# A delta-rule kernel's triangular inverse: from 128x128 products to 64x64 tiles on the array's diagonal

## The chip, the core and the metric

The kernel runs on one core of a Trainium2 chip. The core has a matrix engine (TensorE, PE in the profile, with its weight loads listed apart as PEld), three engines for elementwise work (VectorE or DVE, ScalarE or ACT, GpSimd or POOL) and queues that issue DMAs (here all on SyncE, SP). Each engine works through its own instructions in order, and semaphores tie the engines together. The metric is the device time of one execution in microseconds (us).

## The reference

Four batch elements, eight heads, 768 tokens, 48 values a head. First a delta rule runs along the tokens of each head, with a state S of 48x48 that starts at zero:

```
k_n = k / (norm(k) + 1e-6)
for t in tokens:
    y[t]  = q[t] @ S
    S     = S + beta[t] * outer(k_n[t], v[t] - k_n[t] @ S)
```

The heads' outputs, put side by side, form x of 768x384 for each batch element. Two mixers follow: h = relu(x^T @ w_tok1) @ w_tok2 along the tokens (256 hidden), u = x + h^T, and out = u + relu(u @ w_ch1) @ w_ch2 along the channels (1536 hidden). The mixers' weights come as doubles; everything is computed in float32.

## The kernel before

**The delta rule in chunks.** The 768 tokens of a batch element are cut into six chunks of 128, 24 chunks in all. In a chunk with start state S0, with kb = beta k and L the strictly lower triangle of kb k^T (128x128 for each head), the kernel solves (I + L) u = beta v - kb S0, and then y = q S0 + tril(q k^T, -1) u and S1 = S0 + k^T u.

**The inverse.** T = (I + L)^-1 is built by doubling. With T right for diagonal blocks of s, blocks of 2s follow from T <- T - T L_off T, where L_off holds the blocks below the diagonal that join two blocks of s. The matrix engine takes its left operand (the stationary one, loaded as weights) transposed, so both T (tile t_t) and its transpose W (tile w_t) are kept, 128 partitions by 8 heads by 128 columns. The grams lie in gm, where gm[:, h, 0] is L transposed.

**prep(t)**, lines 237 to 351, does what needs no state. It scales the keys (lines 244 to 268), transposes keys, queries and scaled keys on the matrix engine (p_t, line 276), forms the grams (p_g, line 288, two row tiles of 64 partitions, one for even and one for odd heads) and masks them on DVE into gm (line 292). For blocks of 2, POOL fills w_t with the identity (line 303), masks the gram into off (line 307) and subtracts (line 311); eight transposes (p_w, line 318) and two ACT copies (line 319) make t_t from w_t. Then comes a loop over s = 2, 4, 8, 16, 32, 64. Each step multiplies L by the first-half columns of T (p_l, line 330, eight heads, 128x128 weights against 64 columns), masks the product on DVE into lt (line 331), multiplies lt by the second-half columns of W (p_wu, line 339), and w_t by lt (p_x, line 343, not in the last step), and subtracts the products on DVE from t_t (line 344) and w_t (line 347). A step's p_l waits for the update of t_t of the step before, and p_wu for lt.

**recur(t)**, lines 353 to 407, walks the chunk through the state: p_b, p_u (which reads w_t), p_s, the state's update, p_y. **mixer(b)**, lines 409 to 471, does both mixers of a batch element once its six chunks are done: p (line 416), p_h (428), transposes p_ut (439), p_c (450) with a relu on ACT (455), p_o (462), and the result's addition and DMA (469, 470). **load_weights** rounds the doubles to float32 in 34 pieces, with five or six DVE operations and one POOL addition (line 190) a piece.

**The order.** Each of these functions is a generator that yields between pieces. A heap (lines 480 to 507) takes the pieces by due time: a chunk's preparation takes the unit of time before its recurrence, and a batch element's mixers are spread over the six units after its last chunk. So the first six chunks have no mixer beside them, the other 18 have, and the last batch element's mixer stands alone at the end. The framework's scheduler takes that order as a priority and may move an instruction ahead of one whose inputs it does not expect in time; each engine's order is then fixed in the program. PSUM tiles come from three rings: att (three slots: p_t, p_g, p_w, p_l, p_wu, p_x), seq (two) and mlp (three).

Of the kernel before, what the change touches and what calls it, by code (L numbers as in the profile page):

```python
# [9 lines left out]
FP32 = mybir.dt.float32  # L10
# [4 lines left out]
C = 128   # tokens in a chunk  # L15
DP = 64   # partitions a head takes in the transposed keys and queries
WP = 384  # weights of a partition that are rounded at a time
# [3 lines left out]
def kernel(  # L21
# [24 lines left out]
    on the chip to the nearest float32, the widest type its engines multiply.  # L46
    """
    nc = tc.nc
# [11 lines left out]
    GT = 256            # tokens in a group of the channel mixer  # L60
# [13 lines left out]
    def ps_att(shape, name):  # L74
        return psum.tile(shape, FP32, name=name, tag="att", bufs=3)
# [22 lines left out]
    mask_1 = const.tile([128, 64], FP32, name="mask_1")  # L98
    nc.gpsimd.memset(mask_1, 1.0)
    for sign in (1, -1):  # L100
        nc.gpsimd.affine_select(
            out=mask_1, in_=mask_1, pattern=[[-2 * sign, 64]], base=0,
            channel_multiplier=sign, compare_op=ALU.is_ge, fill=0.0,
        )
    # the other steps, on L T: rows in the second half of their own block of 2s
    SIZES = [2, 4, 8, 16, 32, 64]
    masks = {}
    for s in SIZES:
        m = const.tile([128, 64 // s, s], FP32, name=f"mask_{s}")
# [9 lines left out]
        masks[s] = m  # L119

    # masked L T of a step; the first-half columns are written, the rest stay 0
    lt_buf = {}
    for s in SIZES[:-1]:
        lt_buf[s] = const.tile([128, H, 128], FP32, name=f"lt_{s}")
# [12 lines left out]
    # state, two heads to a block-diagonal block  # L137
# [99 lines left out]
    def prep(t):  # L237
        """What needs no state: scaled keys, masked grams and the inverse."""
# [64 lines left out]
        nc.gpsimd.tensor_copy(  # L303
            out=w_t, in_=ident[:, None, :].to_broadcast([128, H, 128])
        )
        off = work.tile([128, H, 64], FP32, name="off", bufs=1)
        nc.gpsimd.tensor_tensor(  # L307
            out=off, in0=gm[:, :, 0, 1::2],
            in1=mask_1[:, None, :].to_broadcast([128, H, 64]), op=ALU.mult,
        )  # L310
        nc.gpsimd.tensor_tensor(  # L311
            out=w_t[:, :, 1::2], in0=w_t[:, :, 1::2], in1=off, op=ALU.subtract
        )
        yield
        for g in range(H // 4):
            p_t = ps_att([128, 4, 128], "p_w")
            for i in range(4):
                nc.tensor.transpose(p_t[:, i], w_t[:, 4 * g + i], ident)  # L318
            nc.scalar.copy(t_t[:, 4 * g : 4 * g + 4], p_t)
        yield  # L320

        for s in SIZES:
            last = s == SIZES[-1]
            lt = lt_buf[s]
            lt_e = lt[:, :, None, :] if last else pairs(lt, s)[:, :, :, 0]
            t_e = pairs(t_t, s)[:, :, :, 0]
            w_o = pairs(w_t, s)[:, :, :, 1]
            p_l = ps_att([128, H, 64], "p_l")
            for h in range(H):
                nc.tensor.matmul(p_l[:, h], gm[:, h, 0], t_e[:, h])  # L330
            nc.vector.tensor_tensor(  # L331
                out=lt_e, in0=halves(p_l, s),
                in1=masks[s][:, None].to_broadcast([128, H, 64 // s, s]), op=ALU.mult,
            )
            yield
            rows = 64 if last else 128
            p_w = ps_att([rows, H, 64], "p_wu")
            for h in range(H):
                nc.tensor.matmul(p_w[:, h], lt[:, h], w_o[:, h])  # L339
            if not last:  # L340
                p_x = ps_att([128, H, 64], "p_x")
                for h in range(H):
                    nc.tensor.matmul(p_x[:, h], w_t[:, h], lt_e[:, h])  # L343
                nc.vector.tensor_tensor(  # L344
                    out=t_e, in0=t_e, in1=halves(p_x, s), op=ALU.subtract
                )
            nc.vector.tensor_tensor(  # L347
                out=w_o[:rows], in0=w_o[:rows], in1=halves(p_w, s), op=ALU.subtract
            )
            yield  # L350
        ready[t] = (kp, kbq_t, gm, w_t, bv)

    def recur(t):
        """The chunk's walk through the state."""
# [54 lines left out]
    def mixer(b):  # L409
        """Both mixers on a batch element; xb is x, then u = x + h."""  # L410
# [62 lines left out]
    # ---- order of issue: a chunk's recurrence beside the next chunk's  # L473
    # preparation and the mixers of the batch element before ----
# [20 lines left out]
    n_prep = 1 + 3 + H // 4 + 2 + 2 * len(SIZES)  # L495
# [42 lines left out]
```

## Time and profile before

| what | value |
|---|---|
| median of 3 runs | 1697.59 us (1691.23 to 1698.04) |
| the profiled execution, first to last instruction | 1689.6 us |
| PE busy, with 10350 matmuls | 1588.7 us |
| PEld busy, with 10350 weight loads | 1395.2 us |
| DVE busy | 513.9 us |
| ACT busy | 176.7 us |
| POOL busy | 173.8 us |
| mean granted clock of PE | 0.917 |

The profiled execution is known by its span alone; what lies around the span is in the runs' times. A row of a group reads: line of the kernel, engine, operation, output tile <- input tiles, shape, count, then busy time in us and mean ns of one, then the idle time of the engine just before and what ended most of it. For a matmul 128*64 128x64 means 128 weight rows by 64 weight columns, and 64 moving columns on 128 partitions. A row of the order in time reads: start in us, length in us from the first start to the last end, engine, line, operation, tiles, shape, count. The length of one matmul in the trace includes its way through the array, so it is longer than the distance between two starts. The granted clock is 1.00 at full speed.

### The profile page before, as it was taken

How to read it: one execution, taken by the hardware profiler on the slowest of the kernel's cores; microseconds unless marked ns; L12 is line 12 of the kernel's file. 1: busy time of each engine (PE TensorE's matmuls, PEld its weight loads, DVE VectorE, ACT ScalarE, POOL GpSimd, SP SyncE). 2: the span in 40 equal slices, each digit the busy share in tenths (PEclk: the TensorE clock that was granted, in tenths of full speed). 3: DMA queues.
4: the chain of work that ended last, by engine and by line, in shares of the span. 5: the costliest groups of instructions: out<-in, count | busy, mean ns of one | idle time of the engine just before them, and what ended most of it. 6: DMA issues, size and time to landing. Idle time of an engine off the chain costs nothing.

```text
span 1689.6 us, 22914 instructions
## 1 busy us (share of the span) xinstructions
PE 1588.7 (94%) x10350; PEld 1395.2 (83%) x10350; DVE 513.9 (30%) x920; ACT 176.7 (10%) x407; POOL 173.8 (10%) x188
## 2 busy tenths in 40 slices
PE   5888989889899999999999999999999999999999
PEld 4888888888888988888888889879878879888776
DVE  6464643212123232223223222222233232222100
ACT  1000101001011101101100101110110101010111
POOL 5031211001011011101100100110110110000000
PEclk9995757567589999999999999999999999999999
DMA  4131210000000000001000000010000000000000
GB/s 115 38 77 45 71 47 15 5 10 19 0 6 20 5 15 15 10 11 24 11 15 10 15 15 10 15 24 6 15 20 5 10 10 1 6 5 1 10 10 19
DMA packets 83377, 33.02 MB, mean 20 GB/s; under 512 B 75824, under 2 KB 78896, under 8 KB 83280
## 3 DMA queue, kind: packets, MB, share of 16 engines
q1 hardware_dynamic: 83280, 31.56, 7.6%
q8 instruction: 81, 1.33, 0.3%
q14 instruction: 16, 0.13, 0.0%
HBM read 26.84 MB, written 4.72 MB: 19 GB/s over the span
## 4 chain that ended last, share of the span: by engine, by line
PE 90%; DVE 5%; POOL 3%; issue 1%; ACT 0%; POOLq 0%; DVEq 0%
PE p_l L330 18%; PE p_wu L339 17%; PE p_x L343 15%; PE p_o L462 11%; PE p_c L450 10%; PE p_g L288 3%; PE p_u L372 3%; PE p_y L402 2%; PE p_t L276 2%; PE p_h L428 2%; DVE gm L292 2%; PE p L416 1%; PE p_w L318 1%; DVE lt L331 1%; DVE t_t L344 1%; POOL off L307 1%
## 5 line engine op out<-in xcount | busy, mean ns | idle before, releaser
L330 PEld LDWEIGHTS p_l<-t_t,gm 128*128 128x128 f32 x2304 | 316.9, 218 | 54.0 <-DVE t_t L344 37.4
L330 PE MATMUL p_l<-t_t,gm 128*128 128x64 f32 x2304 | 326.4, 302 | 23.5 <-DVE t_t L344 23.1
L339 PEld LDWEIGHTS p_wu<-w_t,lt 128*128 128x128 f32 (+1 forms) x2304 | 297.4, 210 | 57.2 <-DVE lt L331 42.8
L339 PE MATMUL p_wu<-w_t,lt 128*128 128x64 f32 (+1 forms) x2304 | 306.6, 295 | 25.7 <-DVE lt L331 25.7
L343 PE MATMUL p_x<-lt,w_t 128*128 128x64 f32 x1920 | 277.4, 306 | 0.0
L343 PEld LDWEIGHTS p_x<-lt,w_t 128*128 128x128 f32 x1920 | 267.4, 223 | 0.0
L344 DVE TENSOR_TENSOR t_t<-t_t,p_x 128x512 f32<-128x512 f32 x120 | 82.5, 687 | 505.9 <-PE p_x L343 505.9
L450 PE MATMUL p_c<-u_t,wc 128*128 128x256 f32 x864 | 217.1, 388 | 0.1
L462 PE MATMUL p_o<-wc,r 128*128 128x384 f32 x576 | 208.1, 494 | 0.0
L331 DVE TENSOR_TENSOR lt<-p_l,mask 128x512 f32<-128x512 f32 x144 | 99.5, 691 | 325.6 <-PE p_l L330 325.6
L450 PEld LDWEIGHTS p_c<-u_t,wc 128*128 128x128 f32 x864 | 153.1, 190 | 20.2 <-issue 2.6
L462 PEld LDWEIGHTS p_o<-wc,r 128*128 128x128 f32 x576 | 101.5, 191 | 49.7 <-issue 1.3
L347 DVE TENSOR_TENSOR w_t<-w_t,p_wu 128x512 f32<-128x512 f32 x144 | 97.9, 680 | 33.0 <-PE p_wu L339 33.0
L292 DVE TENSOR_TENSOR gm<-p_g,mask_u 128x512 f32<-128x512 f32 x96 | 61.9, 685 | 112.3 <-PE p_g L288 111.9
L455 ACT ACTIVATE r<-p_c 128x256 f32<-128x256 f32 x144 | 55.3, 384 | 385.8 <-PE p_c L450 385.8
L265 POOL TENSOR_TENSOR bv<-v_raw,beta_t 128x384 f32<-128x384 f32 x24 | 20.2, 843 | 654.7 <-DVE rhs L367 497.6
L288 PE MATMUL p_g<-kbq_t,k_t 64*128 64x256 f32 x384 | 61.9, 412 | 9.8 <-DVE gm L292 6.7
L277 ACT COPY k_t<-p_t 128x512 f32<-128x512 f32 x24 | 14.0, 585 | 490.4 <-PE p_t L276 489.9
L288 PEld LDWEIGHTS p_g<-kbq_t,k_t 64*128 64x128 f32 x384 | 38.9, 191 | 26.1 <-DVE gm L292 10.5
L318 PE MATMUL p_w<-ident,w_t 128*128 128x128 f32 x192 | 26.9, 285 | 28.5 <-POOL w_t L311 28.5
L190 POOL TENSOR_TENSOR w_f<-w_f,w_r 128x384 uint32<-128x384 uint32 (+1 forms) x34 | 35.7, 1050 | 171.4 <-DVE w_f L182 166.7
L318 PEld LDWEIGHTS p_w<-ident,w_t 128*128 128x128 f32 x192 | 21.5, 144 | 38.1 <-POOL w_t L311 36.8
(75 smaller groups left out, 967.2 us busy)
## 6 DMA issues: line engine op xcount, KB each, us to landing
d<-in_moe_w_ch_dram SPq DMA_DIRECT2D x24, 384.0 KB, 3.1
k_raw<-in_k_dram SPq DMA_DIRECT2D x24, 192.0 KB, 2.5
qpad<-in_q_dram SPq DMA_DIRECT2D x24, 192.0 KB, 2.8
v_raw<-in_v_dram SPq DMA_DIRECT2D x24, 192.0 KB, 2.6
out_dram<-o_sb SPq DMA_DIRECT2D x24, 192.0 KB, 1.9
d<-in_moe_w_tok_dram SPq DMA_DIRECT2D x6, 256.0 KB, 3.3
d<-in_moe_w_tok_dram SPq DMA_DIRECT2D x4, 384.0 KB, 3.1
beta_sb<-in_beta_dram SPq DMA_DIRECT2D x1, 96.0 KB, 2.2
```

Source lines behind the costliest of these rows:

```text
L288: nc.tensor.matmul(p_g[par][:, jj], k_t[lo : lo + DP, j], kbq_t[lo : lo + DP, j])
L292: nc.vector.tensor_tensor(out=gm[:, 4 * g + par : 4 * g + 4 : 2], in0=p_g[par], in1=mask_u[:, None, None, :].to_broadcast([128, 2, 2, 128] ...
L318: nc.tensor.transpose(p_t[:, i], w_t[:, 4 * g + i], ident)
L330: nc.tensor.matmul(p_l[:, h], gm[:, h, 0], t_e[:, h])
L331: nc.vector.tensor_tensor(out=lt_e, in0=halves(p_l, s), in1=masks[s][:, None].to_broadcast([128, H, 64 // s, s]), op=ALU.mult,)
L339: nc.tensor.matmul(p_w[:, h], lt[:, h], w_o[:, h])
L343: nc.tensor.matmul(p_x[:, h], w_t[:, h], lt_e[:, h])
L344: nc.vector.tensor_tensor(out=t_e, in0=t_e, in1=halves(p_x, s), op=ALU.subtract)
L347: nc.vector.tensor_tensor(out=w_o[:rows], in0=w_o[:rows], in1=halves(p_w, s), op=ALU.subtract)
L450: nc.tensor.matmul(p_c, wc1[:, cb, f * 128 : (f + 1) * 128], u_t[:, cb], start=(cb == 0), stop=(cb == NCB - 1),)
L455: nc.scalar.activation(r, p_c, ACTF.Relu)
L462: nc.tensor.matmul(p_o, r2[f][:, i * C : (i + 1) * C], wc2[:, f], start=(f == 0), stop=(f == NHT - 1),)
```

## The change

The tile size R = 64 is introduced. Up to s = 16, and in the step at s = 32, every product is taken as two 64x64 products, one on partitions 0 to 63 and one on 64 to 127, which write the same partitions of the output. The operands are kept compact: w_r and t_r hold, for each partition, only the 64 columns of its own diagonal block (8 heads by 64), and the masks, the identity and the lt buffers are folded to that width at the start by POOL. T is no longer updated by a product of its own: before each step t_r is made from w_r by a DVE transpose in blocks of 32x32 (flip). The first transposes on the matrix engine and their ACT copies go. The step at 64 is written out: one more product (p_x) and a subtraction make the first block's T complete, then p_l is evacuated by ACT into lt_buf[64] and p_w by ACT, times -1, into the upper right block of w_t. The other blocks of w_t are a POOL memset of zero and two POOL copies of w_6, which is w_r. Comments are dropped, and the count of pieces in the plan follows the new pieces (20, as before).

```diff
+    def folded(name, full, width):
+        t = const.tile([128, width], FP32, name=name)
+        nc.gpsimd.tensor_copy(out=t, in_=full[:, 0:width])
+        for lo in range(width, full.shape[-1], width):
+            nc.gpsimd.tensor_tensor(
+                out=t, in0=t, in1=full[:, lo : lo + width], op=ALU.add
+            )
+        return t
...
-        w_t = work.tile([128, H, 128], FP32, name="w_t")
-        t_t = work.tile([128, H, 128], FP32, name="t_t", bufs=1)
+        w_r = work.tile([128, H, R], FP32, name="w_r", bufs=1)
+        t_r = work.tile([128, H, R], FP32, name="t_r", bufs=1)
         nc.gpsimd.tensor_copy(
...
+        for lo in range(0, 128, R):
+            nc.gpsimd.tensor_tensor(
+                out=off[lo : lo + R], in0=gm[lo : lo + R, :, 0, lo + 1 : lo + R : 2],
+                in1=mask_1[lo : lo + R, None, :].to_broadcast([R, H, R // 2]),
+                op=ALU.mult,
+            )
...
-        for g in range(H // 4):
-            p_t = ps_att([128, 4, 128], "p_w")
-            for i in range(4):
-                nc.tensor.transpose(p_t[:, i], w_t[:, 4 * g + i], ident)
-            nc.scalar.copy(t_t[:, 4 * g : 4 * g + 4], p_t)
-        yield
...
+        def flip(dst, src):
+            nc.vector.transpose(
+                dst.rearrange("p h n -> p (h n)"), src.rearrange("p h n -> p (h n)")
+            )
+
+        def step(s, size, w, t):
+            lt, half = lt_buf[s], size // 2
+            lt_e = pairs(lt, s)[:, :, :, 0]
+            t_e = pairs(t, s)[:, :, :, 0]
+            w_o = pairs(w, s)[:, :, :, 1]
+            p_l = ps_att([128, H, half], "p_l")
             for h in range(H):
-                nc.tensor.matmul(p_l[:, h], gm[:, h, 0], t_e[:, h])
+                for lo in range(0, 128, size):
+                    r = slice(lo, lo + size)
+                    nc.tensor.matmul(p_l[r, h], gm[r, h, 0, r], t_e[r, h])
             nc.vector.tensor_tensor(
                 out=lt_e, in0=halves(p_l, s),
...
+            p_w = ps_att([128, H, half], "p_wu")
             for h in range(H):
-                nc.tensor.matmul(p_w[:, h], lt[:, h], w_o[:, h])
-            if not last:
-                p_x = ps_att([128, H, 64], "p_x")
-                for h in range(H):
-                    nc.tensor.matmul(p_x[:, h], w_t[:, h], lt_e[:, h])
-                nc.vector.tensor_tensor(
-                    out=t_e, in0=t_e, in1=halves(p_x, s), op=ALU.subtract
-                )
+                for lo in range(0, 128, size):
+                    r = slice(lo, lo + size)
+                    nc.tensor.matmul(p_w[r, h], lt[r, h], w_o[r, h])
...
+        for s in SMALL:
+            if s == 32:
+                break
+            flip(t_r, w_r)
+            yield from step(s, R, w_r, t_r)
+        flip(t_r, w_r)
+        if R == 64:
+            w_6, t_6 = w_r, t_r
...
+        yield from step(32, 64, w_6, t_6)
+        lo_r, hi_r = slice(0, 64), slice(64, 128)
+        p_x = ps_att([64, H, 32], "p_x")
+        for h in range(H):
+            nc.tensor.matmul(p_x[:, h], w_6[lo_r, h], lt_buf[32][lo_r, h, 0:32])
+        nc.vector.tensor_tensor(
+            out=t_6[lo_r, :, 0:32], in0=t_6[lo_r, :, 0:32], in1=p_x, op=ALU.subtract
+        )
+        w_t = work.tile([128, H, 128], FP32, name="w_t")
+        nc.gpsimd.memset(w_t[hi_r, :, 0:64], 0.0)
+        nc.gpsimd.tensor_copy(out=w_t[lo_r, :, 0:64], in_=w_6[lo_r])
+        nc.gpsimd.tensor_copy(out=w_t[hi_r, :, 64:128], in_=w_6[hi_r])
+        yield
+        p_l = ps_att([128, H, 64], "p_l")
+        for h in range(H):
+            nc.tensor.matmul(p_l[hi_r, h], gm[lo_r, h, 0, hi_r], t_6[lo_r, h])
+        nc.scalar.copy(lt_buf[64][hi_r], p_l[hi_r])
+        yield
+        p_w = ps_att([64, H, 64], "p_wu")
+        for h in range(H):
+            nc.tensor.matmul(p_w[:, h], lt_buf[64][hi_r, h], w_6[hi_r, h])
+        nc.scalar.mul(w_t[lo_r, :, 64:128], p_w, -1.0)
+        yield
         ready[t] = (kp, kbq_t, gm, w_t, bv)
```

More of the change, by code (lines that the diff above doesn't have):

```diff
@@ L16 @@
 DP = 64
+R = 64
 WP = 384
@@ L118 @@
         )
-        masks[s] = m
+        width = (R if s < R else 64) // 2
+        masks[s] = folded(f"mask_{s}", m.rearrange("p n s -> p (n s)"), width)
+    half_of = const.tile([128, 2], FP32, name="half_of")
+    for i in range(2):
+        nc.vector.tensor_reduce(
+            out=half_of[:, i : i + 1],
+            in_=ident.rearrange("p (n two s) -> p n two s", two=2, s=32)[:, :, i],
+            axis=mybir.AxisListType.XY, op=ALU.add,
+        )
     lt_buf = {}
-    for s in SIZES[:-1]:
-        lt_buf[s] = const.tile([128, H, 128], FP32, name=f"lt_{s}")
+    for s in (2, 4, 8, 16, 32):
+        width = R if s < R else 64
+        lt_buf[s] = const.tile([128, H, width], FP32, name=f"lt_{s}")
         nc.gpsimd.memset(lt_buf[s], 0.0)
@@ L298, in prep @@
             yield
-        w_t = work.tile([128, H, 128], FP32, name="w_t")
-        t_t = work.tile([128, H, 128], FP32, name="t_t", bufs=1)
+        w_r = work.tile([128, H, R], FP32, name="w_r", bufs=1)
+        t_r = work.tile([128, H, R], FP32, name="t_r", bufs=1)
         nc.gpsimd.tensor_copy(
-            out=w_t, in_=ident[:, None, :].to_broadcast([128, H, 128])
+            out=w_r, in_=ident_r[:, None, :].to_broadcast([128, H, R])
         )
-        off = work.tile([128, H, 64], FP32, name="off", bufs=1)
@@ L313, in prep @@
+        nc.gpsimd.tensor_tensor(
+            out=w_r[:, :, 1::2], in0=w_r[:, :, 1::2], in1=off, op=ALU.subtract
         )
         yield
-        for g in range(H // 4):
-            p_t = ps_att([128, 4, 128], "p_w")
-            for i in range(4):
-                nc.tensor.transpose(p_t[:, i], w_t[:, 4 * g + i], ident)
-            nc.scalar.copy(t_t[:, 4 * g : 4 * g + 4], p_t)
-        yield
[L322 to L328, printed above, removed]
+        def flip(dst, src):
+            nc.vector.transpose(
+                dst.rearrange("p h n -> p (h n)"), src.rearrange("p h n -> p (h n)")
+            )
@@ L331, in prep @@
             nc.vector.tensor_tensor(
                 out=lt_e, in0=halves(p_l, s),
-                in1=masks[s][:, None].to_broadcast([128, H, 64 // s, s]), op=ALU.mult,
+                in1=halves(masks[s][:, None, :], s).to_broadcast(
+                    [128, H, half // s, s]
+                ),
+                op=ALU.mult,
             )
             yield
-            rows = 64 if last else 128
-            p_w = ps_att([rows, H, 64], "p_wu")
+            p_w = ps_att([128, H, half], "p_wu")
@@ L347, in prep @@
             nc.vector.tensor_tensor(
-                out=w_o[:rows], in0=w_o[:rows], in1=halves(p_w, s), op=ALU.subtract
+                out=w_o, in0=w_o, in1=halves(p_w, s), op=ALU.subtract
             )
             yield
+        for s in SMALL:
[6 more added lines that the diff above has]
+            w_6, t_6 = w_r, t_r
+        else:
+            w_6 = work.tile([128, H, 64], FP32, name="w_6", bufs=1)
+            t_6 = work.tile([128, H, 64], FP32, name="t_6", bufs=1)
+            for i in range(2):
+                c_i = slice(32 * i, 32 * i + 32)
+                nc.gpsimd.tensor_scalar_mul(w_6[:, :, c_i], w_r, half_of[:, i : i + 1])
+                nc.gpsimd.tensor_scalar_mul(t_6[:, :, c_i], t_r, half_of[:, i : i + 1])
```

23 lines of the change are left out of this document (11 added, 12 removed).

## The prediction

> **What bounds the kernel now.** I read the engines' busy times first, then the span cut where the mixers begin and end, then the groups by tile shape, and last the order of time inside one chunk in each stretch.
>
> ```profile
> span 1689.6 us, 22914 instructions
> PE 1588.7 (94%) x10350; PEld 1395.2 (83%) x10350; DVE 513.9 (30%) x920; ACT 176.7 (10%) x407; POOL 173.8 (10%) x188
> ```
> ```profile
> 42.80:484.00 441.20, 391.81 (x2096) 371.02 (x2098) 172.85 (x331) 24.85 (x51) 60.65 (x56) 0.68 0.12 32
> 484.00:1558.00 1074.00, 1048.11 (x7675) 916.70 (x7673) 305.60 (x514) 124.74 (x291) 89.78 (x84) 1.00 0.05 12
> ```
> (Columns: stretch, length, busy time and count of PE, PEld, DVE, ACT, POOL, then the granted clock, DMA share, GB/s.) TensorE bounds both stretches. From the first p_l at 42.8 us to 484 us the first six chunks run with no mixer beside them at a mean clock of 0.68; until 1558 us the other 18 run beside the mixers at 1.00, with 26 us of PE idle time in all. The last mixer follows and is not touched.
>
> ```profile
> L330 PE MATMUL p_l<-t_t,gm 128*128 128x64 f32 x2304 | 326.4, 302 | 23.5 <-DVE t_t L344 23.1 <-ACT t_t L319 0.3
> L343 PE MATMUL p_x<-lt,w_t 128*128 128x64 f32 x1920 | 277.4, 306 | 0.0
> L339 PE MATMUL p_wu<-w_t,lt 128*128 128x64 f32 x1920 | 274.1, 304 | 21.0 <-DVE lt L331 21.0
> L339 PE MATMUL p_wu<-w_t,lt 128*64 128x64 f32 x384 | 32.4, 248 | 4.7 <-DVE lt L331 4.7
> L318 PE MATMUL p_w<-ident,w_t 128*128 128x128 f32 x192 | 26.9, 285 | 28.5 <-POOL w_t L311 28.5
> ```
> These five rows are the inverse: 937 of the 1589 busy us. 2304 in L330 is 24 chunks x 6 sizes x 8 heads x 2: a float32 matmul is two weight loads and two matmuls.
>
> One step of the first stretch, the change of chunk, and the same step beside the mixers:
>
> ```profile
> 160.85 3.68 PE L330 MATMUL p_l<-t_t,gm 128*128 128x64 f32 x16 [0.78 <-DVE t_t L344]
> 165.31 3.68 PE L339 MATMUL p_wu<-w_t,lt 128*128 128x64 f32 x16 [0.78 <-DVE lt L331]
> 168.78 3.62 PE L343 MATMUL p_x<-lt,w_t 128*128 128x64 f32 x16
> 173.18 3.68 PE L330 MATMUL p_l<-t_t,gm 128*128 128x64 f32 x16 [0.78 <-DVE t_t L344]
> 177.64 1.97 PE L339 MATMUL p_wu<-w_t,lt 128*64 128x64 f32 x16 [0.78 <-DVE lt L331]
> 179.54 1.12 PE L276 MATMUL p_t<-ident,kpad 128*128 128x128 f32 x4
> ...
> 191.31 1.09 PE L318 MATMUL p_w<-ident,w_t 128*128 128x128 f32 x8
> ...
> 192.69 2.00 PE L330 MATMUL p_l<-t_t,gm 128*128 128x64 f32 x16
> ```
> ```profile
> 900.03 1.90 PE L339 MATMUL p_wu<-w_t,lt 128*128 128x64 f32 x16
> 901.76 1.95 PE L343 MATMUL p_x<-lt,w_t 128*128 128x64 f32 x16
> 903.55 1.51 PE L428 MATMUL p_h<-r,w 128*128 128x384 f32 x4
> 904.89 1.89 PE L330 MATMUL p_l<-t_t,gm 128*128 128x64 f32 x16
> 906.62 1.51 PE L428 MATMUL p_h<-r,w 128*128 128x384 f32 x4
> ...
> 938.88 1.15 PE L339 MATMUL p_wu<-w_t,lt 128*64 128x64 f32 x16
> 939.96 0.70 PE L450 MATMUL p_c<-u_t,wc 128*128 128x256 f32 x2
> ```
> In the first stretch a step takes 173.18 - 160.85 = 12.3 us, with PE waiting 0.78 us for DVE twice. Beside the mixers the waits are filled. All three groups move 64 columns; the last p_wu loads 64 weight columns in place of 128 and takes 1.15 us against 1.90. So a group is paid by its weight columns.
>
> **The clock.** It falls with the inverse alone on PE:
>
> ```profile
> 180.00:190.00 10.00, 10.00 (x66) 9.08 (x65) 8.14 (x16) 2.24 (x4) 4.70 (x5) 0.83 0.36 100
> 190.00:200.00 10.00, 9.98 (x80) 9.11 (x79) 9.94 (x17) 2.18 (x5) 5.73 (x5) 1.00 0.35 84
> 200.00:210.00 10.00, 8.44 (x47) 8.30 (x48) 5.69 (x13) 0.00 (x0) 1.00 (x1) 0.69 0.23 75
> 370.00:380.00 10.00, 8.44 (x39) 8.06 (x39) 1.98 (x3) 0.00 (x0) 0.00 (x0) 0.50 0.00 0
> ```
> If the clock is either 0.5 or 1, these means put the rise at 183.4 us and the fall at 203.8 us: full clock from 4 us to 24.3 us after the chunk's first transpose at 179.54, half clock after.
>
> [...]
>
> **The change, part by part.** (1) Up to size 16 and in the step at 32, each 128x128 product becomes two 64x64 products on the array's diagonal, with 64 weight columns and 32 moving ones: 2 tiles x 8 heads x 2 = 32 matmuls a group. (2) p_x goes from every step but the one at 32, where it is 16 matmuls on 64 rows; so do the chunk's 8 transposes (L318) and their two ACT copies. (3) In their place DVE transposes 128x512 once before each of the five steps, on the chain. (4) DVE works on 128x256 instead of 128x512. (5) The step at 64 becomes two groups of 16 matmuls of 64x64, with two ACT evacuations. So 184 matmul calls a chunk for 144, each with half the weight columns.
>
> Whether the two diagonal tiles run at once decides the price. The gram p_g is the one place where two row tiles (64 rows each) follow each other:
>
> ```profile
> 944.18 0.38 PE L450 MATMUL p_c<-u_t,wc 128*128 128x256 f32 x1
> 944.49 0.49 PE L288 MATMUL p_g<-kbq_t,k_t 64*128 64x256 f32 x2
> ```
> ```profile
> 944.49 1.13 PE L288 MATMUL p_g<-kbq_t,k_t 64*128 64x256 f32 x8
> ```
> ```profile
> 1590.78 15.54 PE p_c L450 x72
> ```
> The first pair of rows is an answer cut off at 944.50 us: two p_g matmuls had already started. Eight of 256 columns take 1.13 us in all, while p_c's 256 columns on the whole array come every 15.54 / 72 = 0.216 us, 1.73 for eight. So tiles in different rows overlap here. I take a pair at one weight load of 64 columns: a group of 16 pairs costs what 16 such matmuls cost, 1.15 us at full clock and 1.97 at half. The other bound is no overlap, 32 in a row: about 1.89 and 3.68, the old group's rows.
>
> [...]
>
> DVE, ACT and POOL prices:
>
> ```profile
> L331 DVE TENSOR_TENSOR lt<-p_l,mask 128x512 f32<-128x512 f32 x144 | 99.5, 691 | 325.6 <-PE p_l L330 325.6
> L432 DVE TENSOR_TENSOR xb<-xb,p_h 128x384 f32<-128x384 f32 x24 | 13.3, 554 | 21.0 <-PE p_h L428 20.5
> L319 ACT COPY t_t<-p_w 128x512 f32<-128x512 f32 x48 | 25.9, 588 | 64.8 <-PE p_w L318 57.0 <-issue 6.9 <-ACT ksq L245 0.9
> L307 POOL TENSOR_TENSOR off<-gm,mask 128x512 f32<-128x512 f32 x24 | 31.2, 1300 | 102.7 <-DVE gm L292 102.7
> ```
> 128 columns less cost 0.137 us, so 256 take 0.42. The DVE transpose is not in the trace; I take the 128x512 row, 0.69, between half (0.35) and double (1.38). An ACT evacuation takes 0.59. POOL's off becomes two of 64x256, about 0.65 each, the same 1.3 in sum. Its three new operations at the chunk's end (a memset, two copies to w_t) release only the recurrence, which starts behind the next chunk's transposes; uncovered, three of half the POOL row's size would cost some 2 us a chunk.
>
> Gap after p_l: 0.78 - 0.69 + 0.42 = 0.51. Gap after p_w: 0.51 + 0.69 for the transpose = 1.20; nothing but the chain's next group waits for it. A step is 2 x 1.97 + 1.71 = 5.65 at half clock and 2 x 1.15 + 1.71 = 4.01 at full. The chunk's end is p_x 1.97, gap 0.51, p_l 1.97, gap 0.68 (ACT), p_w 1.97: 7.1.
>
> **First stretch.** The same place of two chunks:
>
> ```profile
> 284.97 3.69 PE p_l L330 x16
> ...
> 359.20 3.69 PE p_l L330 x16
> ```
> 74.2 us a chunk; the first chunk's inverse is 441.2 - 5 x 74.2 = 70.2. After: the first is 0.69 + 5 x 5.65 + 7.1 = 36. The others: the head, 192.69 - 179.54 = 13.15, loses the transposes and copies (192.69 - 191.31 = 1.4) and gains 0.69 for the first transpose: 12.5. Until 24.3 us the clock is full: 11.8 / 4.01 = 2.9 steps; 2.1 more at 5.65 make 11.6; the end 7.1; 43.0 together. 36 + 5 x 43 = 251 us, 190 saved. The weights' rounding keeps DVE up to 9.94 of 10 us busy (190 to 200 us) and now lies beside shorter steps: I charge 10 us, bounds 0 and 30. Stays 180.
>
> **Beside the mixers.** The shortest of one p_wu matmul is the tail that a group's length holds beyond its starts:
>
> ```profile
> L339 PE MATMUL p_wu<-w_t,lt x109: 219/275/323, 900.0 to 960.0; 128*128 128x64 f32 x93, 128*64 128x64 f32 x16
> ```
> 1074 / 18 = 59.7 a chunk. The inverse, start to start: 6 p_l x 1.73, 5 p_wu x 1.73, 5 p_x x 1.79, the last p_wu 1.08, the transposes 1.09 less the tail, 0.9: 30.0; all else 29.7. After: ten groups of 16 pairs and three of 16 singles at 0.058 each ((1.15 - 0.22) / 16) make 12.1. A change of tile shape costs: p_c to p_g takes 944.49 - 944.18 = 0.31 instead of 0.216, so 0.09 in; and 939.96 - 938.88 = 1.08 less 16 x 0.058 leaves 0.15 out. Twelve more such groups: 2.9 (bounds 1.5, half of it lying in waits, and 2.9). The waits on DVE come to some 10 us a chunk, as before (11 x 0.78), and were covered by mixer matmuls; cover for shorter groups is less even, so I charge 2.5, bounds 0 and 5. 29.7 + 12.1 + 2.9 + 2.5 = 47.2, so 12.5 x 18 = 225 saved.
>
> **Sum.** The folded masks add POOL operations ahead of the first chunk, shorter memsets take some away: 1 us, bounds 0 and 4. 1689.6 - 180 - 225 + 1 = 1286 us of span. The median shown, 1697.6, lies 8 us above the profiled span: **1294 us**.
>
> **Rivals.** Middle: pairs overlap only partly, because issue or evacuation can't follow. For it speaks that the trace has no run of small pairs; against it the two starts within 0.02 us. Halfway between 1294 and the next case's 1549: 1422.
>
> No overlap, and the change does not do what it says: groups of 3.68 and 1.89. A step takes 9.07 and 5.49; chunks 53 and 57, so 102 - 10 saved; beside the mixers 160 x 0.058 = 9.3 more a chunk, so 3.2 x 18 = 58. 1690 - 92 - 58 + 9 = 1549. [...]
>
> Slower than before: the clock falls beside the mixers, as it does in the first stretch, because less of the array is in use. At half clock 44.7 us of PE work a chunk takes twice as long, so a chunk is 47.2 + 44.7 x share. It decides from 47.2 + 44.7 x share = 59.7 + 180 / 18, a share of 0.5; at two thirds it is 77 a chunk, 1690 - 180 + 18 x 77 - 1074 + 9 = 1831 us. Against it: what is not inverse rises from 29.7 of 59.7 us (50%) to 29.7 of 47.2 (63%), and that mix held 1.00.
>
> **How the numbers follow.** Chances: forecast 0.70, middle 0.14, no overlap 0.10, clock 0.05, gain lost to waits 0.01. Low end: no weight delay (-10), no uncovered waits (-45), shape changes half hidden (-25), a transpose at half (-10): 1204, taken as 1200. High end: weights 30, double transpose and 5 us of waits give 1294 + 20 + 21 + 45 = 1380; the middle case with half of these and a little more 1480. Left out are no overlap, the clock and the edges, 0.2. A change of 0.5% can just be told from none here; faster 0.93, same 0.02, slower 0.05.
>
> **What would show it.** Right: tiled matmuls starting in pairs a few ns apart, groups of 16 pairs near 1.15 us at full clock, first-stretch chunks near 43 us, 47 beside the mixers, a transpose near 0.69, 1.00 held from the first mixer on. Wrong: groups of 32 near 1.9 us, a clock under 1.00 beside the mixers, or a chunk's gaps well over 10 us.

## The result, and the profile after

| | before | after |
|---|---|---|
| median | 1697.82 us (1691.23 to 1710.52) | 1277.38 us (1268.81 to 1278.84) |
| ratio to before | | 0.751 [0.7469, 0.7552] |
| the profiled execution's span | 1689.6 us | 1276.8 us |
| mean granted clock of PE | 0.917 | 0.908 |

The forecast was 1294 us, 1.3% above the median. In this document a ratio leaves out runs more than 1.5% above the fastest of their kernel; where the clock itself makes a kernel's runs differ (e1, e3, e4, e9 to e12), that also removes slow clocks, so all runs' times are given.

The page of the changed kernel: span, busy times, the granted clock in 40 slices, and the groups that answer to the five rows of the inverse.

```profile
span 1276.8 us, 27386 instructions
PE 1169.6 (92%) x12462; PEld 920.6 (72%) x12462; DVE 431.3 (34%) x898; ACT 180.7 (14%) x407; POOL 197.0 (15%) x295
PEclk9986575776999999899897998999799999799999
L359 PE MATMUL p_l<-t_r,gm 64*64 64x32 f32 x3840 | 157.3, 238 | 65.0 <-DVE t_r L345 60.0
L372 PE MATMUL p_wu<-w_r,lt 64*64 64x32 f32 x3840 | 160.6, 240 | 14.0 <-DVE lt L360 14.0
L345 DVE STREAM_TRANSPOSE t_r<-w_r 128x512 f32<-128x512 f32 x120 | 85.2, 710 | 45.6 <-POOL w_r L338 43.2
L360 DVE TENSOR_TENSOR lt<-p_l,mask 128x256 f32<-128x256 f32 x120 | 50.9, 424 | 175.2 <-PE p_l L359 175.0
```

The inverse's main groups hold PE for 157 and 161 us where three held it for 326, 277 and 274. TensorE is still the bound (92%). The transposes on DVE take 85 us, and PE's wait for them is the largest idle item, 60 of the 65 us before p_l.

The stretches of the changed kernel (columns as in the prediction): first p_l to the seventh chunk, the 18 chunks beside mixers, the last mixer, and five chunks alone. (A few matmuls of the first mixer's p run before the cut at 308.3 us, the first at 76.9.)

```profile
23.50:308.30 284.80, 221.84 (x2654) 200.06 (x2654) 158.76 (x351) 25.93 (x52) 69.52 (x81) 0.71 0.20 54
308.30:1144.80 836.50, 810.80 (x9282) 623.73 (x9281) 250.03 (x497) 128.93 (x293) 108.19 (x157) 0.96 0.07 15
1144.80:1276.80 132.00, 127.78 (x497) 90.17 (x496) 7.79 (x14) 18.78 (x49) 0.00 (x0) 1.00 0.03 12
60.00:260.00 200.00, 157.57 (x1812) 140.92 (x1811) 116.38 (x251) 17.65 (x36) 52.79 (x61) 0.66 0.21 57
```

| | predicted | measured | difference |
|---|---|---|---|
| ahead of the first p_l | 42.8 + 1 | 23.5 | -20.3 |
| six chunks alone, weights | 251 + 10 | 284.8 | +23.8 |
| 18 chunks beside mixers | 18 x 47.2 = 850 | 836.5 | -13.5 |
| last mixer | 131.6 | 132.0 | +0.4 |
| span | 1286 | 1276.8 | -9.6 |

So that the total is right to 1.3% is partly luck, since errors cancel: one by a misreading, one by the weights, one by waits and the clock. The forecast added 8 us from span to median; here the median is 0.6 us above the span, and this is the rest of the 17 us by which it was high.

The order on PE in the changed kernel: the first p_l, one step at half clock, the chunk's end and the next chunk, then a group at full clock beside the mixers, and last the first two starts of such a group, an answer cut off at 642.115 us.

```profile
23.51 1.92 PE L359 MATMUL p_l<-t_r,gm 64*64 64x32 f32 x32 [4.59 <-DVE t_r L345]
...
287.99 1.92 PE L359 MATMUL p_l<-t_r,gm 64*64 64x32 f32 x32 [1.36 <-DVE t_r L345]
290.42 1.92 PE L372 MATMUL p_wu<-w_r,lt 64*64 64x32 f32 x32 [0.52 <-DVE lt L360]
293.70 1.92 PE L359 MATMUL p_l<-t_r,gm 64*64 64x32 f32 x32 [1.36 <-DVE t_r L345]
...
305.52 1.11 PE L301 MATMUL p_t<-ident,kpad 128*128 128x128 f32 x4
...
642.10 1.12 PE L359 MATMUL p_l<-t_r,gm 64*64 64x32 f32 x32
```
```profile
642.10 0.25 PE L359 MATMUL p_l<-t_r,gm 64*64 64x32 f32 x2
```

Two matmuls start within 15 ns (that they are the two tiles of a pair, and not the two halves of one float32 product, is shown by e1, where the same 32 matmuls in another order take 1.84 us, some 58 ns each), and 32 matmuls take 1.12 us at full clock and 1.92 at half: the price of 16 (forecast 1.15 and 1.97). The step takes 293.70 - 287.99 = 5.71 us (forecast 5.65), with waits of 0.52 and 1.36 (0.51 and 1.20).

The group at 23.51 has the length of half clock, while the granted clock reads 9 (90% or more) in the page's first two slices, to 64 us: the clock's column is not to be trusted there, and the lengths of groups are. So 0.66 for 60 to 260 us is rather too high.

### The profile page after: what moved, and what is told of

It is laid out like the page before. It is cut to its first block, busy times and chain, and to the rows that moved or that the text cites. A ratio compares the mean times of both kernels' runs of the same rounds, so it can differ in the third digit from the quotient of the medians.

```text
span 1276.8 us, 27386 instructions
## 1 busy us (share of the span) xinstructions
PE 1169.6 (92%) x12462; PEld 920.6 (72%) x12462; DVE 431.3 (34%) x898; ACT 180.7 (14%) x407; POOL 197.0 (15%) x295
## 4 chain that ended last, share of the span: by engine, by line
PE 86%; DVE 8%; POOL 4%; issue 2%; ACT 0%; POOLq 0%; ACTq 0%
PE p_c L517 15%; PE p_o L529 15%; PE p_l L359 12%; PE p_wu L372 12%; PE p_g L313 4%; PE p_u L439 4%; PE p_y L469 4%; PE p_h L495 3%; PE p_t L301 3%; PE p_l L410 2%; PE p_wu L415 2%; PE p L483 2%; DVE t_r L345 2%; PE p_x L399 2%; POOL off L333 2%
## 5 line engine op out<-in xcount | busy, mean ns | idle before, releaser
L359 PEld LDWEIGHTS p_l<-t_r,gm 64*64 64x64 f32 x3840 | 144.3, 155 | 111.4 <-issue 89.4
L359 PE MATMUL p_l<-t_r,gm 64*64 64x32 f32 x3840 | 157.3, 238 | 65.0 <-DVE t_r L345 60.0
L372 PEld LDWEIGHTS p_wu<-w_r,lt 64*64 64x64 f32 x3840 | 146.5, 158 | 56.7 <-DVE lt L360 33.0
L372 PE MATMUL p_wu<-w_r,lt 64*64 64x32 f32 x3840 | 160.6, 240 | 14.0 <-DVE lt L360 14.0
L360 DVE TENSOR_TENSOR lt<-p_l,mask 128x256 f32<-128x256 f32 x120 | 50.9, 424 | 175.2 <-PE p_l L359 175.0
L373 DVE TENSOR_TENSOR w_r<-w_r,p_wu 128x256 f32<-128x256 f32 x120 | 50.6, 421 | 158.8 <-PE p_wu L372 158.6
L345 DVE STREAM_TRANSPOSE t_r<-w_r 128x512 f32<-128x512 f32 x120 | 85.2, 710 | 45.6 <-POOL w_r L338 43.2
L313 PEld LDWEIGHTS p_g<-kbq_t,k_t 64*128 64x128 f32 x384 | 41.1, 198 | 20.3 <-DVE gm L317 6.5
L469 PE MATMUL p_y<-u,gm 128*128 128x48 f32 x384 | 52.1, 289 | 0.0
L469 PEld LDWEIGHTS p_y<-u,gm 128*128 128x128 f32 x384 | 50.0, 207 | 1.9 <-issue 1.0
L333 POOL TENSOR_TENSOR off<-gm,mask 64x256 f32<-64x256 f32 x48 | 36.0, 750 | 78.0 <-DVE gm L317 76.5
```

What stands on the lines that cost most here:

```text
L313: nc.tensor.matmul(p_g[par][:, jj], k_t[lo : lo + DP, j], kbq_t[lo : lo + DP, j])
L333: nc.gpsimd.tensor_tensor(out=off[lo : lo + R], in0=gm[lo : lo + R, :, 0, lo + 1 : lo + R : 2], in1=mask_1[lo : lo + R, None, :].to_broadc ...
L345: nc.vector.transpose(dst.rearrange("p h n -> p (h n)"), src.rearrange("p h n -> p (h n)"))
L359: nc.tensor.matmul(p_l[r, h], gm[r, h, 0, r], t_e[r, h])
L360: nc.vector.tensor_tensor(out=lt_e, in0=halves(p_l, s), in1=halves(masks[s][:, None, :], s).to_broadcast([128, H, half // s, s]), op=ALU.mult,
L372: nc.tensor.matmul(p_w[r, h], lt[r, h], w_o[r, h])
```

## The experiments

**Theory.** About half of the gain comes from the pairs that run at once, the rest from transposes in place of the product p_x. The first stretch is a chain at half clock with the weights' rounding on DVE beside it. Rivals: the pairs do not matter and fewer products do it all; the clock, not the chain, sets the first stretch.

**e1: the order of the pairs.** All eight heads of one diagonal tile, then all of the other; nothing else.

```diff
-            for h in range(H):
-                for lo in range(0, 128, size):
+            for lo in range(0, 128, size):
+                for h in range(H):
```

> The changed kernel, but in the groups of the five steps all eight heads of the first diagonal tile are issued before those of the second. If the two tiles overlap only because they alternate in the order of issue, a group of 32 matmuls goes back from 1.12 to about 1.9 us at full clock and from 1.92 to about 3.7 at half: beside the mixers 10 x 0.8 us a chunk, 18 chunks, about 145 us; in the first six chunks about 60 groups of 0.8 to 1.8 us, some 80 us; in all about 1500 us. Rival: the array starts whatever tile is free, whatever the order, and the time stays at 1277 within 1%.

Measured: 1749.67 us (1724.79 to 1798.96), ratio 1.0204 [1.0121, 1.0287]. Its order on PE at full and at half clock, and its stretch beside the mixers:

```profile
589.95 1.84 PE L359 MATMUL p_l<-t_r,gm 64*64 64x32 f32 x32
...
598.38 3.22 PE L359 MATMUL p_l<-t_r,gm 64*64 64x32 f32 x32
```
```profile
500.00:1570.00 1070.00, 1045.66 (x8410) 828.20 (x8409) 224.93 (x449) 115.89 (x263) 96.53 (x140) 0.77 0.05 11
```

The same 32 matmuls now take 1.84 us at full clock against 1.12, so here the pairs overlap only where neighbours in the queue use different tiles. That price alone was expected to give some 1500. The rest, some 225 us in the profiled run of 1724.79 us, is mostly the clock. An estimate from its mean, if it is either 0.5 or 1: 0.77 over 1070 us is (1 - 0.77) / 0.5 x 1070 = 492 us at half, which cost about 246, where the changed kernel's 0.96 over 836.5 us cost 33. So the rival that the prediction held for slower than before is real in e1, where the small tiles run one after the other.

**e2: the transposes alone.** The kernel before, with t_t made by a DVE transpose of 128x1024 ahead of each step up to 32, p_x only at 32, and no first transposes on PE; no 64x64 tiles.

```diff
-        for g in range(H // 4):
-            p_t = ps_att([128, 4, 128], "p_w")
-            for i in range(4):
-                nc.tensor.transpose(p_t[:, i], w_t[:, 4 * g + i], ident)
-            nc.scalar.copy(t_t[:, 4 * g : 4 * g + 4], p_t)
-        yield
...
+            if s <= 32:
+                nc.vector.transpose(
+                    t_t.rearrange("p h n -> p (h n)"), w_t.rearrange("p h n -> p (h n)")
+                )
...
-            if not last:
+            if s == 32:
```

> The kernel before, with one part of the change: t_t comes from w_t by a DVE transpose of 128x1024 ahead of each of the steps 2 to 32, so the eight transposes on the matrix engine and the products p_x of the steps 2 to 16 go; the products stay 128x128. The price list says: beside the mixers 4 x 1.79 + 0.9 = 8 us a chunk less, 145 us; in the first six chunks p_x goes but the transpose of some 1.3 us stands on the chain, 2 us a step less, some 50 us; in all about 1500 us. Rival: the longer wait on DVE is not covered beside the mixers, and half of the gain is lost: about 1600 us.

Measured: 1510.17 us (1507.1 to 1521.14), ratio 0.8902 [0.8855, 0.895]. Its transposes and its stretch beside the mixers:

```profile
L317 DVE STREAM_TRANSPOSE t_t<-w_t 128x1024 f32<-128x1024 f32 x120 | 149.1, 1243 | 30.6 <-POOL w_t L311 28.2
```
```profile
450.00:1372.00 922.00, 913.88 (x6318) 773.91 (x6318) 371.55 (x527) 106.87 (x256) 92.14 (x85) 1.00 0.06 14
```

Of the 420 us, 188 come with the transposes and the products that they spare, and the other 233 only with the 64x64 tiles and what goes with them. Here the clock is 1.00 beside the mixers, with products on 128 rows; with the tiles of the changed kernel it is 0.96.

**e3: tiles of 32x32** up to size 16 (four at once), with POOL widening the operands for the step at 32.

```diff
-R = 64
+R = 32
```

> The changed kernel with R = 32: up to size 16 four tiles of 32x32 on the diagonal in place of two of 64x64, operands half as wide, and four POOL operations that widen w_r and t_r ahead of the step at 32. If four tiles overlap as two do, a group of 64 matmuls is bound by the load of 32 columns, some 0.75 us in place of 1.12 at full clock: 8 x 0.4 = 3 us a chunk beside the mixers, 55 us; in the first chunks shorter DVE operations too, but the POOL operations stand on the chain, some 20 us less in all: about 1200 us. Rival: issue of 128 instructions a group is the bound (about 7 ns from start to start at best, more if the queue cannot be kept full), groups stay at 1.1 us or more and the POOL operations make it slower: 1290 us.

Measured: 1364.13 us (1341.58 to 1399.41), 0.80 of before. The rows: a wait of PE for the widening on POOL, a group at full clock, the widening itself, and the stretch beside the mixers.

```profile
283.60 1.92 PE L359 MATMUL p_l<-t,gm 64*64 64x32 f32 x32 [3.30 <-POOL t L392]
...
307.92 0.72 PE L359 MATMUL p_l<-t_r,gm 32*32 32x16 f32 x64
```
```profile
L391 POOL TENSOR_SCALAR w<-w_r,half_of 128x256 f32<-128x256 f32 x48 | 45.5, 958 | 296.9 <-DVE w_r L373 296.9
```
```profile
300.00:1200.00 900.00, 834.06 (x13416) 618.24 (x13416) 203.56 (x487) 124.89 (x281) 164.80 (x258) 0.83 0.06 15
```

The expected 1200 us was missed. The price of a group was right, 0.72 us and so 0.4 cheaper, and issue did not hold it at the rival's 1.1 us, but the kernel is about 87 us slower. Two things stand against it: POOL's widening on the chain (the wait of 3.30 us above), and a clock of 0.83 over 900 us, by the same estimate 306 us at half, which cost some 153. In these kernels the clock beside the mixers holds the less, the smaller the tiles (1.00 in e2, 0.96, 0.83); how much of e3's loss is due to the waits for POOL was not tested apart.

**e4: the clock of the first stretch.** Extra matmuls that nobody reads fill the waits of the first six chunks: the identity as weights, 256 columns after p_l, twice 512 after p_wu (once at 32).

```diff
+        def warm(src, n):
+            if b == 0:
+                p_d = ps_mlp([128, n], "p_d")
+                nc.tensor.matmul(
+                    p_d, ident, src.rearrange("p h n -> p (h n)")[:, 0:n]
+                )
...
+            warm(t, 256)
...
+            for _ in range(2 if s < 32 else 1):
+                warm(lt, 512)
```

> The changed kernel; in the first six chunks dense matmuls whose result nobody reads (256 columns behind p_l, twice 512 behind p_wu, once at size 32) stand in the waits for DVE. [...]

Measured: 1242.8 us (1236.6 to 1256.92), ratio 0.7312 [0.7278, 0.7346]. About 1240 us was expected, and 1285 to 1300 if the clock fell all the same. Its five chunks alone:

```profile
60.00:260.00 200.00, 187.55 (x2317) 139.61 (x2316) 130.51 (x276) 20.28 (x43) 57.70 (x66) 0.93 0.24 62
```

More work makes the kernel faster than the changed one by 1 - 0.7312 / 0.751 = 2.6%: the mean clock of these 200 us goes from 0.66 to 0.93 (in a run of 1256.92 us).

**e5: every transpose done twice**, to see which waits for DVE are covered.

```diff
-            nc.vector.transpose(
-                dst.rearrange("p h n -> p (h n)"), src.rearrange("p h n -> p (h n)")
-            )
+            for _ in range(2):
+                nc.vector.transpose(
+                    dst.rearrange("p h n -> p (h n)"), src.rearrange("p h n -> p (h n)")
+                )
```

> The changed kernel with each DVE transpose done twice, one after the other, on the chain: 0.71 us more in each of five waits of a chunk. If the waits beside the mixers are covered by mixer matmuls, only the first six chunks pay: 6 x 5 x 0.7 = 21 us, about 1298 us, and perhaps some more from a clock that falls a little oftener. Rival: the waits are bare everywhere, 24 x 5 x 0.7 = 85 us, about 1362 us.

Measured: 1284.89 us (1283.86 to 1290.3), ratio 0.7577 [0.7553, 0.76]. Its 18 chunks beside mixers:

```profile
345.00:1150.00 805.00, 792.45 (x9265) 611.53 (x9265) 314.17 (x587) 127.00 (x292) 108.70 (x156) 0.99 0.07 16
```

The first stretch, where the step is a chain, grew: the seventh chunk starts at 340.51 us, not at 305.52. From there to the last p_y the 18 chunks take 817.7 us, 29 less than in the changed kernel (846.6), although DVE does 64 us more there. PE's idle time went from 25.7 to 12.5 us, and the clock from 0.96 to 0.99. So those waits are covered by mixer work even at twice the transpose. With the other wait lengths the scheduler laid out another order; which part of the order keeps the clock was not tested apart. The expected 1298 us came out too high by this gain.

**e6 and e7: the clock with fewer rows or fewer columns in use.** e4's extra matmuls once on 32 of the 128 rows (with all 128 weight columns), once on all rows with 32 of the weight columns. Both use the same quarter of the array, for as many moving columns. The two diffs are against e4.

```diff
-                    p_d, ident, src.rearrange("p h n -> p (h n)")[:, 0:n]
+                    p_d, ident[0:32], src.rearrange("p h n -> p (h n)")[0:32, 0:n]
```

> The run with dense matmuls in the waits of the first six chunks (1243 us), but their operands lie on 32 partitions instead of 128; columns, counts and durations stay. [...]

```diff
-                p_d = ps_mlp([128, n], "p_d")
+                p_d = ps_mlp([32, n], "p_d")
...
-                    p_d, ident, src.rearrange("p h n -> p (h n)")[:, 0:n]
+                    p_d, ident[:, 0:32], src.rearrange("p h n -> p (h n)")[:, 0:n]
```

> The same, but with all 128 rows and only 32 weight columns. Theory (rows count, columns do not): the clock is held as by the full matmuls, about 1243 us. Rival: the used area of the array counts, a quarter here: about 1290 us.

Measured: e6 1363.2 us (1362.53 to 1374.43), ratio 0.8052 [0.8011, 0.8094]; e7 1252.12 us (1245.8 to 1259.76), ratio 0.7379 [0.7338, 0.7421]. The five chunks alone and one step of e6, then of e7:

```profile
60.00:260.00 200.00, 191.71 (x1538) 140.07 (x1537) 109.51 (x243) 16.56 (x32) 52.79 (x57) 0.62 0.22 59
```
```profile
233.08 1.92 PE L366 MATMUL p_l<-t_r,gm 64*64 64x32 f32 x32
...
237.93 3.77 PE L352 MATMUL p_d<-lt,ident 32*128 32x512 f32 x4
241.63 1.92 PE L366 MATMUL p_l<-t_r,gm 64*64 64x32 f32 x32
```
```profile
60.00:260.00 200.00, 187.01 (x2174) 131.42 (x2173) 126.86 (x270) 19.78 (x42) 57.21 (x65) 0.86 0.24 61
```
```profile
252.46 1.12 PE L366 MATMUL p_l<-t_r,gm 64*64 64x32 f32 x32
253.51 0.62 PE L352 MATMUL p_d<-t_r,ident 128*32 128x256 f32 x2
254.11 1.12 PE L380 MATMUL p_wu<-w_r,lt 64*64 64x32 f32 x32
255.16 1.90 PE L352 MATMUL p_d<-lt,ident 128*32 128x512 f32 x4
257.00 1.12 PE L366 MATMUL p_l<-t_r,gm 64*64 64x32 f32 x32
```

In both PE is busy with hardly a gap (191.71 and 187.01 of 200 us), yet in these steps e6 runs at half clock (groups of 1.92; 0.62 over the 200 us) and e7 at full (1.12; 0.86). So idle time does not tell the two apart, nor does the used area, which is the same; the rows in use do. e7 came near the 1243 us expected. For e6 my estimate was about 1290 us if the clock fell to half as in the changed kernel, and 1243 if the rows did not matter. The direction was right and the price wrong: it took 1.7 us for the fills after p_wu at half clock, but each call of 512 columns is two matmuls, and the four take 3.77 us.

**e8: the weights' share.** The loading and rounding of the mixers' weights is replaced by a constant.

```diff
-    at(-0.8, (NCH + 0.6) / (n_pieces + 1), load_weights)
+    def fill_weights():
+        for t in (w1, w2, wc1, wc2):
+            for j in range(t.shape[1]):
+                nc.vector.memset(t[:, j], 0.01)
+
+    at(4.5, 0, fill_weights)
```

> The changed kernel without the loading and rounding of the mixers' weights: they are set to a constant by DVE in the fifth chunk, so the mixers multiply by other numbers. It tells what the rounding costs the chain in the first chunks. The prediction charged 10 us (bounds 0 and 30). By the trace of the changed kernel the waits of a step are 1.5 to 1.7 us with rounding and 1.36 without, so 1 to 2 us a chunk for four chunks, and the second and third chunk have heads of 20 us in place of 12 because the clock rises late; if the rounding is the cause of that too, some 20 us in all: about 1257 us. Rival: the late clock has another cause: about 1270 us.

Measured: 1262.56 us (1262.07 to 1263.35), ratio 0.7439 [0.7421, 0.7457]. Starts of the chunks numbered 1 and 6 in it, and the first p_l of chunk 1:

```profile
61.83 1.11 PE L301 MATMUL p_t<-ident,kpad 128*128 128x128 f32 x4
...
77.58 1.12 PE L359 MATMUL p_l<-t_r,gm 64*64 64x32 f32 x32 [0.52 <-DVE kden L278]
...
289.12 1.11 PE L301 MATMUL p_t<-ident,kpad 128*128 128x128 f32 x4
```

A chunk alone takes (289.12 - 61.83) / 5 = 45.5 us. In the changed kernel the same two starts give 49.3:

```profile
59.18 1.11 PE L301 MATMUL p_t<-ident,kpad 128*128 128x128 f32 x4
...
79.64 1.12 PE L359 MATMUL p_l<-t_r,gm 64*64 64x32 f32 x32
...
305.52 1.11 PE L301 MATMUL p_t<-ident,kpad 128*128 128x128 f32 x4
```

So the rounding costs 3.8 x 5 = 19 us there, 15 in the median. What is left over the forecast's 43.0 is not the weights: a chunk's head in part at half clock (15.8 us in this chunk here, 20.5 in the changed kernel, for 12.5 forecast; p_u in it takes 3.48 us in both, and 1.88 in e1's trace at full clock) and the longer wait for the transpose. The time lies between the forecast (1257) and the rival (1270): chunk 1's late clock is due to the weights only in part.

**e9 to e12: a faster version.** e9 fits the fills to the waits: one call of 512 after p_wu instead of two, 256 in the chunk's end, four of 512 ahead of the first step, and one on gm in each chunk beside the mixers. e10 adds that half of off is formed on DVE. e11 is e4 with that split, and e12 is e11 with e9's fills in the chunk's end.

```diff
+        for _ in range(4 if t == 0 else 1 if b > 0 else 0):
+            warm(gm[:, 4:6].rearrange("p h k n -> p (h k n)"), 512)
...
+            if b == 0:
+                warm(flat(lt), 512 if s < 32 else 256)
```

> The changed kernel with dense matmuls that nobody reads, fitted to the waits: in the first six chunks 256 columns behind p_l and 512 behind p_wu once (0.43 and 0.85 us at full clock, waits of 0.52 and 1.36), 256 in the waits of the chunk's end, four of 512 ahead of the first chunk's first step; beside the mixers one of 512 behind the grams, where p_l waits for off and the clock fell in ten of 18 chunks. [...]

```diff
-            nc.gpsimd.tensor_tensor(
+            (nc.vector if lo else nc.gpsimd).tensor_tensor(
                 out=off[lo : lo + R], in0=gm[lo : lo + R, :, 0, lo + 1 : lo + R : 2],
```

> The same, with one of the two 64x256 operations that make off (0.75 us each, one after the other on POOL) given to DVE, so that both run at once: the wait of p_l at each chunk's start is 0.7 us shorter where it is bare, at most 24 x 0.7 = 17 us under the run beside it; no gain if DVE's queue holds it up as long.

e11 is e4's and e10's diff together:

> The run with twice 512 columns behind p_wu in the first six chunks (1243 us), with off split over POOL and DVE. [...]

```diff
+        warm(w_6, 256)
...
+        warm(t_6, 256)
```

> The same with 256 dense columns in two of the waits of the chunk's end as well, first six chunks only: they fit the wait at full clock, so at worst nothing is lost; if the clock fell there, up to 10 us less: 1220 to 1235 us.

| | all runs, us | median | ratio |
|---|---|---|---|
| e9 | 1243.6 to 1320.63 | 1287.49 | 0.734 [0.7293, 0.7387] |
| e10 | 1231.4 to 1292.34 | 1251.35 | 0.7273 [0.7226, 0.732] |
| e11 | 1242.9 to 1264.54 | 1248.46 | 0.735 [0.7312, 0.7387] |
| e12 | 1228.22 to 1248.14 | 1239.19 | 0.7276 [0.7241, 0.731] |

The five chunks alone of e9 and of e12:

```profile
60.00:260.00 200.00, 186.80 (x2196) 144.59 (x2196) 127.09 (x267) 21.27 (x44) 56.06 (x66) 0.82 0.23 60
```
```profile
60.00:260.00 200.00, 192.15 (x2402) 140.56 (x2400) 136.19 (x283) 22.13 (x47) 55.30 (x64) 0.97 0.23 62
```

e9 missed: some 1200 us expected, 1240 or more if the fills delay the chain by as much as they gain, median 1287. Six runs of one program spread over 77 us, and the mean clock of a run goes with its time, from 0.953 at 1243.6 us to 0.881 at 1320.63; I take it that the thinner fills do not hold the clock every time, which was not tested further. Its expectation also counted ten spells of half clock beside the mixers of the changed kernel, where there are six. The split of off shows no gain clear of the noise: e11 is not faster than e4, and the intervals of e9 and e10 overlap. e11 and e12 missed too (1228 to 1235 and 1220 to 1235 expected). e12 is the fastest median, with the clock at 0.97 in these chunks; against e4 (0.7312 [0.7278, 0.7346]) the intervals overlap. Against the changed kernel's 0.751 both are clearly faster, e12 by 1 - 0.7276 / 0.751 = 3%.

Beside the mixers e9 and e10 show more. They alone have a fill behind the grams, in the wait before a chunk's first p_l. The same stretch of the changed kernel, of e9 and of e10:

```profile
350.00:1100.00 750.00, 725.25 (x8290) 555.66 (x8287) 226.14 (x450) 116.34 (x265) 100.25 (x145) 0.97 0.07 16
350.00:1100.00 750.00, 732.62 (x8370) 554.44 (x8366) 222.05 (x444) 118.90 (x270) 97.37 (x140) 0.99 0.07 16
350.00:1100.00 750.00, 741.62 (x8508) 562.05 (x8507) 234.93 (x465) 122.55 (x278) 87.84 (x126) 1.00 0.07 16
```

Without that fill e4, e11 and e12 have 0.93, 0.96 and 0.94 there (e5, with its other order, 0.99). So a chunk's first wait is where the clock beside the mixers is mostly lost, by one profile of each kernel. The 18 chunks gain little by it: from the seventh chunk's first transpose to the last p_y they take 851 us in e9 and 833 in e10, against 847 in the changed kernel.

## Why the prediction was right, and where it was not

**The pairs overlap: right.** 1.12 and 1.92 us a group; e1 shows that the overlap is bound to the order (1.84 us at full clock in its order). No row of before showed such pairs, so the chance of 0.10 for no overlap was my estimate. The new pairs write two partition halves of one PSUM tile, where the p_g pairs of before write two tiles; the two starts within 15 ns above show that this did not keep them apart here.

**The transpose and DVE: right.** 0.71 us for 0.69, 0.42 for 0.42. e2's 128x1024 takes 1.24.

**Ahead of the first step: a misreading, -20.3 us.** The prediction put the first p_l of before at 42.8 us. That row of before's trace is its second step:

```profile
30.48 3.67 PE L330 MATMUL p_l<-t_t,gm 128*128 128x64 f32 x16
...
42.87 1.54 PE L330 MATMUL p_l<-t_t,gm 128*128 128x64 f32 x6 [0.85 <-DVE t_t L344]
```

The first stretch of before so began at 30.48, and its first chunk had 12.3 us that the prediction left ahead of it; 7 more are that after's first p_l comes at 23.5, with no transposes on PE (8 matmuls, 1.97 us) and their copies ahead of it, which was not split further; the last 1 is the charge for the folded masks.

**Six chunks alone: 24 us short.** The first chunk was right: 36 us, and 59.18 - 23.51 = 35.7 measured. The terms that failed were the weights (10 us charged, 19 by e8, inside the bounds of 0 and 30), the wait for the transpose (1.36 for 1.20), and the clock carried over from before: it was to be full from 4 us after the chunk's first transpose, but chunk 1's head runs at half clock, and its first p_l, 20.5 us after that transpose, is the first group at full length. Of the 24 us the weights are 9, the cut at 308.3 instead of 305.52 is 2.8, and the other two terms together are e8's 5 x (45.5 - 43.0) = 12; they were not split.

**Beside the mixers: 13.5 us too much, by two errors.** The forecast's 47.2 us a chunk held 2.5 for waits without cover. They are covered: PE idles 836.5 - 810.8 = 25.7 us there, as much as the 26 of before, and e5, even with twice the transpose, takes 805 / 18 = 44.7, which is 29.7 + 12.1 + 2.9, the sum without that charge. (That it agrees to the tenth is luck: e5's cuts are round, and a clock of 0.99 took something as well.) But the step that said the clock would hold 1.00 was wrong. At 0.96 over 836.5 us, by the estimate used for e1, 67 us went at half clock and cost about 33, 1.9 a chunk: 44.7 + 1.9 = 46.6 against 836.5 / 18 = 46.5 measured. One such spell of the changed kernel, in slices of 3.4 us, then PE's order and DVE's and POOL's in it:

```profile
523.40:526.80 3.40, 1.65 (x36) 1.20 (x34) 0.71 (x1) 0.38 (x1) 1.42 (x2) 1.00 0.00 0
526.80:530.20 3.40, 3.40 (x38) 3.23 (x38) 1.69 (x4) 0.00 (x0) 0.01 (x1) 0.50 0.02 5
530.20:533.60 3.40, 3.40 (x15) 2.79 (x14) 1.13 (x2) 0.10 (x1) 0.81 (x1) 0.50 0.29 58
533.60:537.00 3.40, 3.40 (x70) 2.61 (x68) 0.42 (x1) 1.08 (x3) 0.00 (x0) 1.00 0.00 0
```
```profile
521.08 2.86 PE L517 MATMUL p_c<-u_t,wc 128*128 128x256 f32 x12
525.69 1.12 PE L359 MATMUL p_l<-t_r,gm 64*64 64x32 f32 x32 [1.75 <-DVE t_r L345]
```
```profile
522.55 1.52 POOL L333 TENSOR_TENSOR off<-gm,mask 64x256 f32<-64x256 f32 x2 [2.47 <-DVE gm L317]
524.16 0.74 POOL L338 TENSOR_TENSOR w_r<-w_r,off 128x256 f32<-128x256 f32 x1
```

Before a chunk's first step, gm, off, w_r and the transpose follow each other on DVE and POOL. Where no mixer matmul is left for that time, PE waits 1.75 us, and the only work after it in that slice is a group of small tiles; the next two slices run at half clock (0.50). All six spells of half clock beside the mixers follow such a wait, of 1.5 to 1.8 us; some waits as long, as at 477 and 814 us (1.84 and 1.75 us), cost no clock. So the rival "the clock falls beside the mixers" came true at a share of 67 / 836.5 = 0.08, far from the 0.5 from which it decides; e1 brings it to 492 / 1070 = 0.46 and is slower than before.

**The clock of the first stretch: right, but for its start.** Past a chunk's head and first steps the forecast had half clock, and a step there takes 5.71 us for 5.65. PE idles no longer than 2.1 us at a time in the five later chunks, and their clock is 0.66.

## What to carry to other kernels

Here two small products on the array's diagonal ran at once, for the price of one (1.12 us for 32 matmuls), only where neighbours in the queue used different tiles (1.84 us in e1), so put the tile loop innermost. Count what a cheaper product does to the clock, too: here, where a chain of small tiles had the clock at 0.66, matmuls that nobody reads, on all 128 rows, brought it to 0.93 and more than paid for themselves (2.6%). Leave some margin: e9's fills, cut to fit the waits, came with an uncertain time (1243.6 to 1320.63 us). And compare a forecast with the result stretch by stretch, since errors of a sum can cancel.

## What the hardware showed that was not expected

In these runs the clock did not go by how busy PE is. The five chunks alone, from 60 to 260 us:

| | PE busy, of 200 us | granted clock |
|---|---|---|
| changed kernel | 157.57 | 0.66 |
| e4, fills of 128 rows by 128 weight columns | 187.55 | 0.93 |
| e6, fills of 32 rows by 128 | 191.71 | 0.62 |
| e7, fills of 128 rows by 32 | 187.01 | 0.86 |

e6 has the busiest PE of the four and the lowest clock, and in before's row from 370 to 380 us PE is busy for 8.44 of 10 us at 0.50. The length of a wait does not tell either: beside the mixers of the changed kernel half clock follows the waits of 1.49 us that end at 619.88 and at 907.70 us, and none follows the one of 1.84 us that ends at 478.96. That fills on 32 rows did not hold the clock, and fills on 32 columns nearly did as well as whole ones, is what these runs show; why the clock goes so stays open.
